# Third batch's attention weights and x turned by 32x32 blocks on VectorE instead of by TensorE, strided x copied in token order, and two weight pieces moved behind the sixth pair's copies

## The chip, the cores and the metric

One core of one Trainium2 chip. The metric is the device time of one execution in microseconds (us). Each time named as a result is a median of several executions; the rows of a profile come from one execution recorded by the hardware profiler.

## The reference

```python
def reference(q, k, v, g_ln, w_ch1, w_ch2):        # q, k, v: (B=8, H=8, S=576, D=64)
    stride = 32
    scores = (1.0 / np.sqrt(D)) * np.matmul(q, k.transpose(0, 1, 3, 2))
    rel = pos[:, None] - pos[None, :]
    mask_local = (rel >= 0) & (rel < stride)                       # heads 0 to 3
    mask_strided = (rel >= 0) & (pos[None, :] % stride == pos[:, None] % stride)   # heads 4 to 7
    scores = np.where(masks, scores, -1e9)
    attn = exp(scores - max); attn = attn / (sum(attn) + 1e-09)
    x = (attn @ v).transpose(0, 2, 1, 3).reshape(B, S, 512)
    mu, var = mean and variance of x over the last axis
    xn = (x - mu) / np.sqrt(var + 1e-06) * g_ln
    return x + np.maximum(xn @ w_ch1, 0.0) @ w_ch2                 # w_ch1: 512x2048, w_ch2: 2048x512
```

All arrays are fp32.

## The kernel before

**Split numbers.** Every operand of the feed-forward part is held as a high and a low part (`xh`/`xl`, `hh`/`hl`, two parts of each weight) in the fp32r format, and a product is three matmuls: high by high, high by low, low by high. The subtraction of the mean is folded into the first weights, and g_ln too.

**The attention** works on pairs of heads. A batch has four pairs, taken in the order local, strided, local, strided; pairs 8 to 11 are the third batch. Because of the masks only small blocks of scores exist: for a local pair 64 keys for each 32 queries, for a strided pair the tokens of one residue class, 18 by 18, in three classes at a time (54). `sm` holds the scores of a pair and later its softmax weights, with the query on the partition. To multiply by `v` the weights are needed with the key on the partition (`pt`), and the result `xo` (query on the partition) is needed with the channel on the partition (`xh`, `xl`) for the feed-forward part.

**Two ways of turning exist already.** Pairs 8 to 11 (`weights_and_x`, L678) are turned by TensorE: transposes of 128x128 tiles into a PSUM bank `px`, from which ScalarE copies `pt` and `xh`, and VectorE makes `xl`. From the fourth batch on the turn goes through DRAM: `spread` (L700) writes `sm` to a buffer `wd`, and `to_blocks` reads it back so that each 32x32 block stands in its final place but not turned; the same for x, which has gone to DRAM in any case (`xdl`, `xds`) and comes back as `sx`. One step of the loop later `turn_blocks` (L724) lets VectorE turn all blocks of a tile by one STREAM_TRANSPOSE; ScalarE makes `xh` from `sx`, VectorE `xl`, and the row sums follow.

**The order of the work.** TensorE runs its instructions in the order in which they are written. The start, about the first 100 us, follows a table, `ORDER`, for the first two batches: a letter and a pair (a, b, c, d of batch one, a1, b1, c1, d1 of batch two; b1 is the sixth pair), or a weight chunk such as `w3.lo0`, with an engine behind a slash where it matters. Here `C` is the copy of turned q or k from PSUM, `S` the scores, `E` the exponential, `P` the transposes of the weights, `F1` a feed-forward product; `w3.lo0` and `w3.sc0` are an ACT, a DVE and again an ACT instruction on half a chunk of w_ch1 (L229, L235).

After the table comes a loop of steps (run, f). A run is a batch with some of the 16 chunks f of the hidden layer: the second batch (`runs[1]`) with all 16, then the first batch with f = 8 to 15 (`runs[2]`), then the batches three to seven. Each step is: the first product of chunk f (L813, 12 matmuls), a slot, and the second product of the chunk before it (L838, 12 matmuls). In a slot the generator `visits` (L1067) may do one piece of attention work. `slots` says which steps have one: for the third batch before, f = 11 and 13 of the second batch's run and all eight steps of the first batch's rest.

A visit belongs to two pairs: the scores and softmax of pair i+1 and the values (product with `v`) of pair i, in one PSUM bank `sv` (`scores_and_values`, L614). For the third batch a visit had two pieces, `scores_and_values` and `weights_and_x`; from pair 12 on it has three: `scores_and_values` with `spread`, a piece with only loads, and `turn_blocks`.

`turn` (behind the second product of a step) turns q and k of the next pair and starts loads of the pair after: `load_half(0)` q, `load_half(1)` k, both on SyncE's queue. From pair 15 on k is loaded by ScalarE's queue behind `turn_blocks` instead.

`x_views` gives the pieces in which `x_high` (ACT, L599) and `x_low` (DVE, L604) copy a turned x. For a strided pair the PSUM bank holds the tokens by residue class, and they must come out in token order.

`x_t` gives two x buffers in turn; the third batch's is the one that the second batch used.

## Time and profile before

| | us |
|---|---|
| median of 3 executions (896.02 to 897.35) | 897.05 |
| the profiled execution | 897.86 |
| span of its records | 896.0 |
| TensorE matmul busy (PE) | 879.9 (98%) |
| VectorE busy (DVE) | 454.9 (51%) |
| ScalarE busy (ACT) | 241.6 (27%) |
| GpSimd busy (POOL) | 239.1 (27%) |

The profiled execution lies 0.81 us above the median; 1.86 us of it lie outside the span. PE is the matmul part of TensorE and PEld its weight load, which overlaps it. SP is SyncE, which mostly issues DMAs; ACTq and SPq are the queues' own records. All times below are microseconds from the start of the span.

### The profile page before, as it was taken

Reading aid. Unit: us, or ns where it says so; the run is one execution under the profiler, and the core shown is the slowest. Engines: PE = TensorE matmul, PEld = TensorE weight load, DVE = VectorE, ACT = ScalarE, POOL = GpSimd, SP = SyncE. Lnnn points to the kernel's source line nnn. Section 1 sums busy time; section 2 is a strip of 40 time slices with the busy share of each in tenths; the row PEclk is TensorE's granted clock in tenths of the full one; section 3 lists DMA queues with packets and bytes.
Section 4 is the critical chain, followed back from the end, with each engine's and each line's share of the span. In section 5 each row is a group of like instructions: output and inputs, shape, how many; then the busy total and the mean of one; then the engine's idle time right before and its main releaser. Section 6 shows DMA issues by size and latency. Waiting matters only on the chain.

```text
span 896.0 us, 18471 instructions
## 1 busy us (share of the span) xinstructions
PE 879.9 (98%) x7467; PEld 723.4 (81%) x7467; DVE 454.9 (51%) x855; ACT 241.6 (27%) x433; POOL 239.1 (27%) x293
## 2 busy tenths in 40 slices
PE   7889999999999999999999999999999999999998
PEld 5778888888888888888888888888888788888886
DVE  5887475346755455544645455546643754232400
ACT  4666465112211111111111111111122443333200
POOL 6768287110100010000100010001000468676000
PEclk9999999999999999999999999999999999999999
DMA  9989891117877565756485758575952001001210
GB/s 210 214 187 254 175 299 37 17 43 181 150 159 118 108 120 108 142 111 121 93 152 102 136 96 170 108 128 108 185 117 81 13 12 48 1 1 43 92 31 24
DMA packets 330973, 100.66 MB, mean 112 GB/s; under 512 B 269712, under 2 KB 321800, under 8 KB 330888
## 3 DMA queue, kind: packets, MB, share of 16 engines
q1 hardware_dynamic: 289704, 93.93, 47.2%
q10 hardware_dynamic: 41184, 5.54, 4.4%
q8 instruction: 59, 0.97, 0.5%
q14 instruction: 26, 0.21, 0.1%
HBM read 72.37 MB, written 27.06 MB: 111 GB/s over the span
## 4 chain that ended last, share of the span: by engine, by line
PE 93%; DMA 4%; SPq 1%; DVE 1%; ACT 1%; issue 0%; ACTq 0%
PE po L838 44%; PE ph L813 33%; PE u L1253 5%; PE sv L659 5%; PE v L1253 2%; DMA s<-in_moe_w_ch_dram 1%; PE c L1253 1%; DMA v_l<-in_v_dram 1%; DMA rows<-in_k_dram 1%; PE px L690 1%; DMA rows<-in_q_dram 1%; PE cm L270 0%; SPq L359 0%; PE pp L498 0%; SPq L412 0%; PE ph L968 0%
## 5 line engine op out<-in xcount | busy, mean ns | idle before, releaser
L838 PE MATMUL po<-w,hh 128*128 128x512 f32 x1024 | 320.3, 394 | 0.0
L813 PE MATMUL ph<-xh,w 128*128 128x512 f32 x880 | 290.5, 391 | 0.0
L838 PEld LDWEIGHTS po<-w,hh 128*128 128x128 f32 x1024 | 188.9, 188 | 39.3
L824 DVE SCALAR_TENSOR_TENSOR hl<-ph,hh 128x512 fp32r<-128x512 f32 x112 | 77.4, 692 | 263.5 <-ACT hh L819 263.5
L838 PE MATMUL po<-w,hl 128*128 128x512 f32 x512 | 199.4, 390 | 0.0
L813 PEld LDWEIGHTS ph<-xh,w 128*128 128x128 f32 x880 | 165.2, 188 | 34.5 <-DVE hl L824 0.2
L813 PE MATMUL ph<-xl,w 128*128 128x512 f32 x440 | 171.2, 389 | 0.0
L819 ACT ACTIVATE hh<-ph 128x512 fp32r<-128x512 f32 x112 | 66.8, 597 | 339.5 <-PE ph L813 298.9
L488 POOL TENSOR_TENSOR sm<-sm,mx 128x640 f32<-128x640 f32 (+1 forms) x32 | 40.6, 1270 | 343.7 <-issue 201.9
L838 PEld LDWEIGHTS po<-w,hl 128*128 128x128 f32 x512 | 96.1, 188 | 20.4
L813 PEld LDWEIGHTS ph<-xl,w 128*128 128x128 f32 x440 | 82.6, 188 | 16.8
L493 ACT ACTIVATE sm<-sm 128x640 f32<-128x640 f32 (+1 forms) x32 | 23.8, 743 | 104.7 <-POOL sm L488 104.7
L780 POOL TENSOR_TENSOR rs<-rs,mhalf 128x1 f32<-128x1 f32 x28 | 15.4, 552 | 121.6 <-DVE rs L779 95.5
L838 PE MATMUL po<-w,h 128*128 128x512 f32 x186 | 42.3, 389 | 0.0
L1120 POOL TENSOR_TENSOR sr<-sr,w 128x256 f32<-128x256 f32 x48 | 40.1, 836 | 3.8
L838 PEld LDWEIGHTS po<-w,h 128*128 128x128 f32 x186 | 34.9, 188 | 7.2
L1120 POOL TENSOR_TENSOR s<-sr,s 128x256 fp32r<-128x256 f32 x32 | 24.8, 803 | 25.3 <-ACT s L1239 25.3
L239 DVE SCALAR_TENSOR_TENSOR p<-s,p 128x512 uint32<-128x512 uint32 x32 | 22.0, 689 | 11.7 <-ACT p L235 11.2
L484 DVE TENSOR_REDUCE mx<-sm 128x10 f32<-128x640 f32 (+1 forms) x32 | 26.3, 823 | 1.9
L1120 DVE TENSOR_TENSOR x<-po,x 128x512 f32<-128x512 f32 x8 | 5.3, 689 | 39.6 <-PE po L838 29.9
L671 DVE TENSOR_TENSOR xo<-sv,den 128x256 f32<-128x256 f32 (+1 forms) x72 | 24.0, 390 | 0.0
L245 DVE SCALAR_TENSOR_TENSOR r<-s,p 128x512 uint32<-128x512 uint32 x32 | 21.9, 686 | 1.6
(195 smaller groups left out, 984.1 us busy)
## 6 DMA issues: line engine op xcount, KB each, us to landing
s<-in_moe_w_ch_dram SPq DMA_DIRECT2D x32, 512.0 KB
out_dram<-x SPq DMA_DIRECT2D x32, 256.0 KB
raw<-in_q_dram SPq DMA_DIRECT2D x104, 72.0 KB
raw<-in_k_dram ACTq DMA_DIRECT2D x68, 72.0 KB
v_l<-in_v_dram SPq DMA_DIRECT2D x32, 144.0 KB
x<-xdl SPq DMA_DIRECT2D x34, 128.0 KB
x<-xds SPq DMA_DIRECT2D x34, 128.0 KB
xdl<-xo SPq DMA_DIRECT2D x16, 256.0 KB
```

Source lines behind the costliest of these rows:

```text
L239: nc.vector.scalar_tensor_tensor(out=self.p[i], in0=self.bits(i), scalar=3, in1=self.p[i], op0=ALU.logical_shift_left, op1=ALU.bitwise_or)
L484: engine(self.mx[:, :, 0:nt], self.smv, axis=AX.X)
L488: nc.gpsimd.tensor_tensor(out=sm, in0=sm, in1=mx[:, :, 0:nt].unsqueeze(3).broadcast_to([P, 2, nt, w]), op=ALU.subtract)
L493: nc.scalar.activation(out=self.smv, in_=self.smv, func=AF.Exp, scale=SCALE)
L659: nc.tensor.matmul(dst, at, by, start=True, stop=True, tile_position=pos)
L671: nc.vector.tensor_tensor(out=xot[0:n, :, t0:t1], in0=src, in1=pv.den[0:n, :, t0:t1].unsqueeze(3).broadcast_to([n, 2, t1 - t0, D]), op=ALU ...
L813: nc.tensor.matmul(ph, w[:, cc], x[:, cc, :], start=(n + k == 0), stop=(n == NCC - 1 and k == 2))
L819: nc.scalar.activation(out=hh, in_=ph, func=AF.Relu)
L824: nc.vector.scalar_tensor_tensor(out=hl, in0=ph, scalar=0.0, in1=hh.bitcast(F32), op0=ALU.max, op1=ALU.subtract)
L838: nc.tensor.matmul(po, hx[:, cs], w, start=(start and n == 0), stop=(stop and n == 2))
L1120: engine.tensor_tensor(out=out, in0=a, in1=b, op=op)
L1253: nc.tensor.matmul(po, a[:, c], b[:, c, :], start=(start and c + k == 0), stop=(stop and c == 1 and k == 2), skip_group_check=True)
```

## The change

Four edits:

1. Pairs 8 to 11 (visits 7 to 11) now go the way of the later pairs: `spread`, and `turn_blocks` in a third piece. `weights_and_x` is gone. The slots become f = 9 to 15 of the second batch's run and the same eight steps behind it: 15 pieces, three a visit, where there were 10.
2. k of pairs 10 to 14 is loaded on ScalarE's queue behind `turn_blocks`, not on SyncE's.
3. `x_views` reads the strided pair's bank with a stride and writes `xh` and `xl` in token order; before it read nearly in order and wrote with a stride. Only the four strided pairs of the first two batches still use it.
4. In `ORDER`, `w3.lo0` and `w3.sc0` stand behind `C.qb1/ACT C.kb1/DVE` and `E.a1`. The rest of the table is the same, with other line ends.

```diff
 ORDER = """
...
-L.c1 w1.lw0 H.d Z.a1/DVE T.b1 w3.lo0 U.a1 Y.d F1.1.b w3.sc0 F1.1.a C.qb1/ACT C.kb1/DVE D.a1/POOL
-F1.0.d E.a1 w3.mg0 S.b1 w1.hi1 w3.sg0 w2.cm L.X4 P.a1 M.b1 w3.lo1 w3.bg F1.1.d L.vb1 G.a1 w2.ce
...
+C.qa1/ACT O.d w2.hi1 S.a1 L.Y3 w1.hi0 R.b1/POOL X.d M.a1 L.c1 w1.lw0 H.d Z.a1/DVE T.b1 U.a1 Y.d F1.1.b
+F1.1.a C.qb1/ACT C.kb1/DVE E.a1 w3.lo0 w3.sc0 D.a1/POOL F1.0.d w3.mg0 S.b1 w1.hi1 w3.sg0 w2.cm L.X4 P.a1
...
                 g = px[:, 0:P * NS].rearrange("p (g x) -> p g x", x=64)[:, :, 0:GS].rearrange(
-                    "p g (s t) -> p g s t", t=NB)[:, :, :, 0:n]
+                    "p g (s t) -> p t g s", t=NB)[:, 0:n]
...
-                    return x[:, cc, :].rearrange("p (t r) -> p r t", r=STR)
+                    return x[:, cc, :].rearrange("p (t r) -> p t r", r=STR)
...
-                if i < 3 * NHP + 2:
+                if i < 2 * NHP + 1:
                     pairs[i + 1].load_half(1)
...
             scores_and_values(pv, p)
-            by_blocks = i >= 3 * NHP
             px = pv if pv and pv.b + 1 < B else None
-            if by_blocks:
-                spread(px, p)
+            spread(px, p)
             turned(i + 2)
-            if by_blocks:
-                yield
+            yield
             if pv and i + 2 < NP:
                 pairs[i + 2].load_v()
             yield
-            (turn_blocks if by_blocks else weights_and_x)(px, p)
-            if by_blocks and i + 3 < NP:
+            turn_blocks(px, p)
+            if i + 3 < NP:
                 pairs[i + 3].load_half(1, nc.scalar)
             yield
...
-    LAST = 7
+    FIRST, LAST = 9, 7
...
-        slots[n] = (r is runs[1] and f in (11, 13) or r is runs[2]
+        slots[n] = (r is runs[1] and f >= FIRST or r is runs[2]
```

**The sixth pair.** On ACT, around the copies of b1's q (`qt_s`), before:

```order
L599 ACTIVATE xh_622<-px_3_867 128x30x16
L599 ACTIVATE xh_622<-px_3_867 128x2x16
L235 ACTIVATE p_3_902<-s_3_776 128x512
L229 ACTIVATE s_3_776<-s_3_776 128x512
L394 COPY qt_s<-t_2_891 128x32x16
L396 COPY qt_s<-tr_2_892 128x2x32
L493 ACTIVATE sm_200<-sm_200 128x2x5x64
L288 ACTIVATE w_1_949<-r_1_668 128x512
```

and now:

```order
L598 ACTIVATE xh_622<-px_3_867 128x16x30
L598 ACTIVATE xh_622<-px_3_867 128x16x2
L393 COPY qt_s<-t_2_891 128x32x16
L395 COPY qt_s<-tr_2_892 128x2x32
L492 ACTIVATE sm_200<-sm_200 128x2x5x64
L234 ACTIVATE p_3_917<-s_3_776 128x512
L228 ACTIVATE s_3_776<-s_3_776 128x512
L287 ACTIVATE w_1_949<-r_1_668 128x512
```

The two instructions on the weight chunk (`p_3`, `s_3`) moved behind three: the two copies of b1's q and the exponential of a1.

**The end of the second batch's run.** On ACT (with the numbers: `hh1_14` is chunk 14 of the second batch, `xh2` the third batch's x, `sm1`/`sm0` the weights of a local or strided pair), before:

```order
L819 ACTIVATE hh1_14_2458<-ph1_14_2445 128x512
L819 ACTIVATE hh1_15_2494<-ph1_15_2481 128x512
L819 ACTIVATE hh0_8_2525<-ph0_8_2512 128x512
L493 ACTIVATE sm0_199<-sm0_199 128x2x6x54
L819 ACTIVATE hh0_9_2637<-ph0_9_2624 128x512
L599 ACTIVATE xh2_2663<-px2_2_2652 128x512
L695 COPY pt2_2_2667<-px2_2_2652 128x768
```

and now:

```order
L796 ACTIVATE hh1_14_2550<-ph1_14_2537 128x512
L706 ACTIVATE xh2_2555<-sx2_0_2458 128x512
L347 DMA raw2_3_2509<-in_k_dram 32x18x32 x4
L796 ACTIVATE hh1_15_2600<-ph1_15_2587 128x512
L492 ACTIVATE sm1_200<-sm1_200 128x2x5x64
L796 ACTIVATE hh0_8_2714<-ph0_8_2701 128x512
```

The first write of `xh2`, with four loads of k behind it, now stands ahead of `hh1_15`; before it stood behind the run's last chunk. Its buffer was the second batch's x, which TensorE reads up to the product `ph1_15`.

What SP issues for the visit after it, now (`xds2` is x on its way to DRAM, `sx2` and `pt2` what comes back):

```order
L553 DMA xds2_213<-xo2_2_2670 54x6x128
L553 DMA xds2_213<-xo2_2_2670 54x5x128
L681 DMA wd1_220<-sm1_200 128x5x128
L699 DMA sx2_2_2677<-xds2_213 32x16x32 x4
L699 DMA pt2_1_2682<-wd1_220 32x20x32 x4
L347 DMA raw3_0_2720<-in_q_dram 32x18x32 x4
```

Of these the rows of `wd1`, `sx2` and `pt2` are new for the third batch, nine DMAs in such a visit.

**A piece of the third batch's weights.** On PE, at f = 9 of the first batch's rest, before:

```order
L813 MATMUL ph_9_2624<-xl_623,w_9_1863 128x512
L813 MATMUL ph_9_2624<-xh_622,w_9_1863 128x512
L690 MATMUL px_2_2652<-ident,xo_0_2594 128x128 x4
L690 MATMUL px_2_2652<-ident,sm_199 128x128 x6
L838 MATMUL po_8_0_2510<-w_8_1813,hh_8_2525 128x512 x2
```

and now at the place of such a piece (f = 14 of the second batch's run), and at the next slot:

```order
L790 MATMUL ph_14_2537<-xl_1066,w_14_2145 128x512
L790 MATMUL ph_14_2537<-xh_1065,w_14_2145 128x512
L815 MATMUL po_0_0_1685<-w_13_2099,hh_13_2503 128x512 x2
...
L790 MATMUL ph_15_2587<-xh_1065,w_15_2188 128x512
L658 MATMUL sv_1_2604<-v_s,pt_2_2463 64x64 x22
L658 MATMUL sv_1_2604<-kt_l,qt_l 32x64 x36
```

The transposes (`px`) are gone from PE, 47 in the five pieces together; the `sv` pieces stand at f = 9, 12 and 15 of the second batch's run and f = 10 and 13 of the first batch's rest. Else PE's order is the same.

## Rows read from the trace of the kernel before

**Rows 1.** The page's first part: busy time, share of the span and instructions of each engine.

```profile
PE 879.9 (98%) x7467; PEld 723.4 (81%) x7467; DVE 454.9 (51%) x855; ACT 241.6 (27%) x433; POOL 239.1 (27%) x293
```

**Rows 2.** The page's chain of work that ended last, shares by engine.

```profile
PE 93%; DMA 4%; SPq 1%; DVE 1%; ACT 1%; issue 0%; ACTq 0%
```

**Rows 3.** The chain, third batch's pieces: start, us, what.

```profile
177.36 0.55 PE px L690 x5
...
201.67 1.09 PE px L690 x10
...
215.65 1.20 PE px L690 x11
```

**Rows 4.** The chain again, around the sixth pair.

```profile
37.90 7.08 DMA s<-in_moe_w_ch_dram
...
45.00 0.62 ACT p L235
...
47.64 0.91 PE sp L457 x44
...
54.90 0.66 PE pp L498 x6
```

**Rows 5.** PE's and ACT's waits from 40 to 48: total, times, longest.

```profile
PE sp L457 <- DVE kt_s L396: 2.3, 1, 2.3
...
ACT p L235 <- DMA s<-in_moe_w_ch_dram: 2.0, 1, 2.0
```

**Rows 6.** Busy time in stretches.

```profile
core 0: us, PE busy (x) PEld busy (x) DVE busy (x) ACT busy (x) POOL busy (x), PEclk, DMA share, GB/s
47.60:52.40 4.80, 4.76 (x131) 3.95 (x134) 4.10 (x7) 2.76 (x5) 3.80 (x5) 0.64 0.79 135
194.10:250.00 55.90, 55.90 (x698) 46.49 (x698) 39.96 (x80) 14.28 (x22) 7.29 (x8) 1.00 0.69 146
602.20:620.50 18.30, 18.30 (x216) 15.01 (x202) 10.51 (x19) 3.06 (x5) 1.26 (x1) 1.00 0.68 133
```

**Rows 7.** Timeline of POOL and ACT around 50: start, us, engine, operation, idle before.

```profile
46.04 2.23 POOL L401 COPY v_l<-v_l 32x1088 f32<-32x1088 f32 x2 [1.75 <-DMA v_l<-in_v_dram]
49.12 1.04 POOL L253 TENSOR_TENSOR wg<-r,gcol 128x512 f32<-128x512 f32 x1 [0.84 <-DVE r L245]
...
51.47 1.27 POOL L488 TENSOR_TENSOR sm<-sm,mx 128x648 f32<-128x648 f32 x1
...
52.78 0.75 ACT L493 ACTIVATE sm<-sm 128x648 f32<-128x648 f32 x1 [0.81 <-POOL sm L488]
```

**Rows 8.** Groups by form, first 105 us: count, busy us, mean ns, idle before.

```profile
L599 ACT ACTIVATE xh<-px 128x480 fp32r<-128x480 f32 x4 | 4.3, 1066 | 1.8 <-PE px L559 1.6
...
L599 ACT ACTIVATE xh<-px 128x512 fp32r<-128x512 f32 x4 | 2.4, 597 | 2.3 <-PE px L559 2.3
L388 ACT COPY kt_l<-t 128x512 f32<-128x512 f32 x3 | 1.8, 594 | 6.7 <-PE t L377 6.7
```

**Rows 9.** Timeline, two visits of a later batch with block turns.

```profile
597.32 0.97 DVE L731 STREAM_TRANSPOSE pt<-pt 128x768 f32<-128x768 f32 x1
...
598.63 4.64 ACTq L348 DMA_DIRECT2D raw<-in_k_dram  x4
...
600.73 0.91 PE L659 MATMUL sv<-v_s,pt 54*64 54x64 f32 x44
...
603.38 0.60 ACT L819 ACTIVATE hh<-ph 128x512 fp32r<-128x512 f32 x1 [5.32 <-DMA v_l<-in_v_dram]
...
617.62 0.84 DVE L731 STREAM_TRANSPOSE pt<-pt 128x640 f32<-128x640 f32 x1 [1.42 <-DMA pt<-wd]
...
619.01 0.97 PE L659 MATMUL sv<-v_l,pt 64*32 64x64 f32 x72
```

**Rows 10.** DVE's waits from 590 to 670.

```profile
DVE pt L731 <- DMA pt<-wd: 5.2, 3, 2.3
```

**Rows 11.** Timeline, loads of k at an earlier visit.

```profile
270.82 2.00 ACTq L348 DMA_DIRECT2D raw<-in_k_dram  x4
```

More of the change, by code (lines that the diff above doesn't have):

```diff
@@ L676, in scores_and_values @@
             pv.x_store(whole=False)
-    def weights_and_x(px, p):
-        ps = bank(f"px{p.id if p else px.id}")
-        n_x = 0
-        turns_x, turns_p = [], []
-        if px:
-            n_x = NT if px.local else NS
-            turns_x = [(t, px.xov[:, t]) for t in range(n_x)]
-        if p:
-            turns_p = [(n_x + t, p.sm[:, t].rearrange("p h x -> p (h x)")) for t in range(p.nt)]
-        k = -n_x % NT
-        for t, src in turns_p[:k] + turns_x + turns_p[k:]:
-            nc.tensor.transpose(ps[:, P * t:P * (t + 1)], src, ident)
-        if px:
-            px.x_parts(ps)
-        if p:
-            p.pt = smp.tile([P, NS, P], F32, tag="pt", name=f"pt{p.id}")
-            nc.scalar.copy(out=p.pt[:, 0:p.nt].rearrange("p t x -> p (t x)"),
-                           in_=ps[:, P * n_x:P * (n_x + p.nt)])
-            p.row_sums()
-            p.inverse()
     def spread(px, p):
```

45 lines of the change are left out of this document (22 added, 23 removed).

## The prediction

> **What bounds the kernel now.** First the page's busy times [rows 1]: TensorE's matmuls fill 98% of the span, no other engine much over half. The chain of work that ended last says the same of its length: 93% PE, the rest almost all in the first hundred microseconds, where the loads set the pace [rows 2]. Next, the place of the change. In the stretch from 194.1 to 250.0, which holds most of the third batch's pieces, PE is busy 55.90 of 55.90 us at a granted clock of 1.00 (of 2.4 GHz), with the DMA engines busy 0.69 [rows 6]. So there a matmul taken off PE's list shortens the run by its own time, and VectorE, busy 39.96 us, and the DMAs cost something only where PE comes to wait for them. Around the sixth pair it is otherwise: PE stands idle for 2.3 us until the copy of `kt_s` is there, and just before, ACT has stood idle for 2.0 us until a weight chunk lands [rows 5]. These are the two places to price. The sum is made for the profiled execution (897.86, span 896.0) and its difference carried to the median, 897.05, 0.81 lower; a difference under 0.2% (1.8 us) I call none, as that is about what a measurement of this kernel can tell.
>
> **Term 1: the transposes.** The 47 px transposes of five pieces stand on the chain as five pieces of it: 0.55 us for five of them, 1.09 for ten, 1.20 for eleven [rows 3]; the last two sizes come twice (two more pieces, like these two). 0.55 + 2 x 1.09 + 2 x 1.20 = 5.13 us. Nothing is put on PE in their place. The `sv` pieces move, but are as many and as long. PE's saving here is **5.1 us**; it could be less only by waits, which are term 4.
>
> **Term 2: the sixth pair.** Before, ACT waits 2.0 us for the weight chunk, whose landing ends 7.08 us of DMA that began at 37.90, does its two instructions (0.62 and about as much), and only then copies b1's q; VectorE copies b1's k after that, and PE's scores of b1 start at 47.64 [rows 4, 5]. With the chunk's two instructions behind, the copies of q and k can go while the chunk is still on its way, and the scores start up to 2.3 us earlier. Behind the idle time the granted clock is 0.64 from 47.6 to 52.4 [rows 6]; at full clock that stretch of 4.8 us would be 4.8 x 0.64 = 3.1, another 1.7 us. So the gain lies between 0 (something else ends last) and 2.3 + 1.7 = 4.0. What is late next is GpSimd: two copies of `v_l`, which wait for a DMA and end at 46.04 + 2.23 = 48.27, three weight instructions that take 51.47 - 49.12 = 2.35 us, b1's subtraction, 1.27 us, and then ACT's exponential, 0.75 us [rows 7]. Packed without a gap they end at 48.27 + 2.35 + 1.27 + 0.75 = 52.64, and b1's weights can be transposed then, at 52.7 in place of 54.90 [rows 4]. I take 54.9 - 52.7 = **2.2 us**. The 2.3 and the 1.7 don't add past this point, because GpSimd's start hangs on a DMA that the change doesn't touch. The moved weight instructions are hardly late: the three that pass them run mostly in the 2.0 us in which ACT waited for the chunk.
>
> **Term 3: x in token order.** Before, a copy of 480 elements a partition takes ACT 1066 ns, one of 512 without a stride on either side 597 [rows 8]; VectorE's copies differ alike. If the stride of the write is what costs, each of the four large copies on each engine gets about 0.47 us shorter. If the strided read costs the same again, nothing is gained; a strided read may also cost more. The nearest row is a copy that reads PSUM with a stride and writes without one (`kt_l`, L388): 594 ns [rows 8]. I go by it. But none of the eight lies on the path: at the only one near it, b1's (d before it), PE's later work waits for loads, and the copies of the other pairs end long before their use. The term is **0**, and up to 1 us either way if the price of a read with a stride is far from that row.
>
> The Trainium skill, "SBUF — State Buffer", section "Door 1: The DMA port swizzle (why `[64,N]` ≈ `[32,N]`)", says the opposite of the row: PSUM is read in lines of 8 bytes, so that an access to it that isn't contiguous slows matmuls down, where SBUF forgives a stride of up to 4 fp32 values. If the rule holds for copies too, edit 3 would move the stride to the dearer side and save nothing; by the row it saves 0.47 us a copy. The sum is the same by either, and L388's 594 ns disagrees with the rule.
>
> **Term 4: the trip through DRAM.** The five visits now take three steps each, and each has a round trip: exponential, write of `sm`, read in blocks, VectorE's turn, which must be done before the next `sv` piece. No visit of the third batch shows it in the trace, but the last batches do it at the same distance of 18.3 us with the DMA engines busy 0.68, nearly the 0.69 here [rows 6]. There the local pair's turn ends at 617.62 + 0.84 = 618.46 and the `sv` piece starts at 619.01: 0.55 us to spare. The strided pair's ends at 597.32 + 0.97 = 598.29, `sv` at 600.73: 2.4 to spare [rows 9]. VectorE does wait for `pt`, three times, 2.3 us at most [rows 10], PE not. So at the later batches' pace the trip costs nothing. VectorE's added turns, 0.84 to 0.97 us each for the weights and no longer for x, which is smaller, have cover: it is busy 40 of 55.9 us in the third batch's stretch [rows 6, 9].
>
> One wait is new. `xh2`'s buffer is read by PE up to `ph1_15`, so at visit 8 ACT stands until that product is done, and behind it stand four loads of k and `hh1_15`; VectorE waits for `xh2`, and the next visit's masking stands behind that. The loads of k take ACT's queue from 2.00 us [rows 11] to 4.64 [rows 9]. ACT's `hh` then starts 0.6 + 2.0 = 2.6 to 0.6 + 4.64 = 5.2 us after `ph1_15`'s end, which is where `sv` starts; at the visit of before it came 603.38 - 600.73 = 2.65 after [rows 9]. The softmax of that visit is so 0 to 2.6 us later than at that visit, and with 0.55 to spare the next `sv` waits 0 to 2.0 us. `hl` is made at the latest 5.2 + 0.6 + 0.7 = 6.5 us after, and PE needs it only behind an `sv` piece of 1.7 and two products of 2.7, 7.1. I take **0.5**, near the lower end, because the loads of k two steps ahead of a busy weight stream look like the short ones.
>
> **Sum.** -5.1 - 2.2 + 0 + 0.5 = -6.8 us. 897.86 - 6.8 = 891.1 for an execution like the profiled one, 897.05 - 6.8 = **890.3** as the median.
>
> **The rivals.**
>
> *The head's gain is given back.* The chain up to there is made of loads of weights, and the share of the DMA engines is 0.79 from 47.6 to 52.4 [rows 6]. If the next chunk sets the time at which PE can go on, the 2.2 us become a wait some microseconds later. Against it: behind 54.90 the chain goes on through PE's own work, not through a load. The time would be 892.5. Chance 0.18.
>
> *A PSUM read with a stride is dear.* Then ACT and VectorE take as long as before or longer in the four pairs; if each of the two pairs whose copies come in this stretch then holds the path up by 0.5 us, the time is 891.3. Chance 0.10.
>
> *The trip is too long (the other side).* The block writes and reads move in pieces of 128 bytes, and with the third batch they come at a time when x of the second batch is fetched and its output is stored. If the trip takes longer than at the later visits by d us, the two local visits cost d - 0.55 each and the two strided d - 2.4 each, 4d - 5.9 in all, and the gain of 7.3 is used up at d = 3.3. At d = 4 it is 10 us, and the time 897.05 - 7.3 + 10.1 = 900. For it: of the three visits of rows 10 one has VectorE wait 2.3 us for `pt`, so the trip has no slack, and SP takes its DMAs in order, `pt` behind the loads of `sx`, which wait for x's own store. Against it: the share of the DMA engines is the same, and the k loads leave SP. Chance 0.22, of which half ends above 898.85.
>
> The Trainium skill, "DMA: Bandwidth & Descriptors", section "Specifications", gives 512 bytes as the least transfer for full rate; the pieces here have 128, which makes this rival a little more likely. The visits of rows 9 make the trip in time with such pieces.
>
> *That the change doesn't do what it says* is excluded for term 1: PE's new order has none of the transposes.
>
> **How the numbers follow.** My own case has 0.50, with a range of its own of 888.0 (head 4.0 in place of 2.2, no wait) to 892.2 (a wait of 2.0, head 1.8). The given-back head 0.18, dear reads 0.10, the long trip 0.22. What leaves out about two in ten is 887.0 to 896.0: below, a head that gains the whole 4.0, no wait and 1 us from the copies; above, the long trip up to d near 3. Faster by over 0.2% (below 895.25): the first three cases, 0.78, and the mild end of the trip, 0.03: 0.81. No difference (895.25 to 898.85): 0.08. Slower: 0.11.
>
> **What would show it.** The rows of px at L690 are gone, and PE is still without a gap from 160 to 250: term 1. PE's wait for `kt_s` at the sixth pair is gone or below 0.5 us, the clock there is nearer 1, and b1's transposes start near 52.7, with no new wait up to 70: term 2; if they come early and a wait for a weight chunk follows, the first rival. Copies `xh` of 480 near 600 ns: term 3; near 1000 or more, the second. PE waits for `pt` at `sv` in the third batch by 0.5 us, in the visit behind `ph1_15` and there alone: term 4; waits at all four, the third rival. The prediction is wrong if the trip is longer than at the later visits, or if what PE gains in the head is not the whole head's gain.

## The result, and the profile after

The changed kernel is slower: 901.39 us against 896.9 in the same runs, a ratio of 1.0058 [1.0038, 1.0078]. The forecast was 890.3. The profiled execution of it took 908.72, 7.3 above its median; 4.3 us of its distance to the profiled execution of before lie in the start, ahead of 97 us, and are not part of what follows.

The page's busy times and the chain by engine, after:

```profile
PE 883.2 (97%) x7420; PEld 724.3 (80%) x7420; DVE 459.4 (51%) x862; ACT 235.0 (26%) x426; POOL 238.7 (26%) x293
...
PE 70%; DMA 2%; DVE 2%; SPq 2%; issue 1%; ACT 1%; POOL 0%; ACTq 0%; DVEq 0%
```

PE has 47 instructions fewer than in [rows 1], as the change says, but it is busy longer, and the chain, 93% PE in [rows 2], is 70%. Busy time by stretches shows where (the columns are those of [rows 6]); first after:

```profile
core 0: us, PE busy (x) PEld busy (x) DVE busy (x) ACT busy (x) POOL busy (x), PEclk, DMA share, GB/s
180.00:250.00 70.00, 64.96 (x599) 52.30 (x598) 42.55 (x85) 10.61 (x17) 8.38 (x10) 0.98 0.82 162
250.00:300.00 50.00, 48.01 (x420) 39.16 (x419) 26.68 (x49) 7.53 (x12) 3.63 (x4) 0.97 0.71 134
...
235.00:245.00 10.00, 6.84 (x62) 5.26 (x50) 5.24 (x13) 0.97 (x2) 1.81 (x2) 0.90 1.05 173
...
243.00:247.00 4.00, 4.00 (x12) 3.10 (x11) 2.21 (x7) 1.33 (x2) 1.51 (x2) 0.57 0.69 215
...
260.00:264.00 4.00, 4.00 (x84) 3.36 (x67) 1.25 (x3) 0.60 (x1) 0.00 (x0) 0.57 0.67 91
```

and before, the same stretch:

```profile
180.00:250.00 70.00, 70.00 (x760) 57.94 (x760) 43.12 (x88) 15.47 (x24) 8.39 (x10) 1.00 0.57 123
```

PE was never idle there and now is for 5.0 + 2.0 = 7.0 us, and behind two of the idle times the granted clock is 0.57 in a stretch of 4 us (243 to 247, 260 to 264), at the lower of its two levels (1.2 of 2.4 GHz) for most of it: 2 x 4 x 0.43 = 3.4 us more. The share of the DMA engines has gone from 0.57 to 0.82; from 194.1 to 250, the stretch of [rows 6], it has gone from 0.69 to 0.84. Between two marks that both kernels have, the last pair of transposes of strided x in the table (93.00, now 97.32) and one in the tail (717.26, now 728.16), it is 630.84 in place of 624.26: 6.6 us longer, though 5.1 us of transposes are gone. So some 11.7 us are lost in that execution, of which idle time and clock explain 10.4; the rest stays unassigned. In the median it is 4.5 + 5.1 = 9.6.

A visit of the third batch in the timeline (start, us, engine, operation, and in brackets the idle time before it and what ended it). It is the visit of pair 11's values and pair 12's scores, the slowest. Pair 12 is the first of the fourth batch, but its weights too were turned by TensorE before:

```profile
233.42 1.11 PE L658 MATMUL sv<-v_s,pt 54*64 54x64 f32 x44 [1.64 <-issue]
...
235.43 4.63 ACTq L347 DMA_DIRECT2D raw<-in_k_dram  x4
...
240.16 0.60 ACT L796 ACTIVATE hh<-ph 128x512 fp32r<-128x512 f32 x1 [9.46 <-DMA raw<-in_k_dram]
...
241.54 0.50 PE L790 MATMUL ph<-xh,w 128*128 128x512 f32 x1 [3.16 <-DVE hl L801]
...
244.21 0.73 SPq L553 DMA_DIRECT2D xds<-xo  x2
...
245.38 0.39 SPq L681 DMA_DIRECT2D wd<-sm  x1
...
250.84 1.90 SPq L699 DMA_DIRECT2D sx<-xds  x4
...
252.84 2.08 SPq L699 DMA_DIRECT2D pt<-wd  x4
...
257.24 0.84 DVE L708 STREAM_TRANSPOSE pt<-pt 128x640 f32<-128x640 f32 x1 [1.74 <-DMA pt<-wd]
...
258.71 0.50 PE L790 MATMUL ph<-xl,w 128*128 128x512 f32 x1 [1.99 <-DVE xl L710]
...
259.38 1.05 PE L658 MATMUL sv<-v_l,pt 64*32 64x64 f32 x72
```

The trip from the `sv` piece to the turned `pt` takes 257.24 + 0.84 - 233.42 = 24.7 us; for the local pair's weights of [rows 9] it was 618.46 - 600.73 = 17.7. Two things are longer. ACT can't make `hh`, which stands behind the loads of k, until 6.7 us after `sv` (2.65 in [rows 9]), so the masking and all behind it are 4.1 us late. And SyncE reads back later. It asks for `pt` 252.84 - 245.38 = 7.5 us behind the store of the weights (`wd`), against 613.55 - 608.68 = 4.9 at the visit of before, and for x 250.84 - 244.21 = 6.6 us behind x's own store, against 611.54 - 607.49 = 4.05 (these rows are of the kernel before):

```profile
582.45 0.97 PE L659 MATMUL sv<-v_l,pt 64*32 64x64 f32 x72
...
607.49 0.73 SPq L554 DMA_DIRECT2D xds<-xo  x2
...
608.68 0.39 SPq L704 DMA_DIRECT2D wd<-sm  x1
...
611.54 1.90 SPq L722 DMA_DIRECT2D sx<-xds  x4
...
613.55 2.07 SPq L722 DMA_DIRECT2D pt<-wd  x4
```

4.1 + 2.6 are 6.7 of the 7.0. The second part is mostly the landing: in the trace the store of the weights has landed 6.4 us after its issue, where it took 3.7 at the visit of before, and `pt` is asked for 1.1 us after that.

The first part comes from how the two queues are tied together. The DMAs of SyncE and ScalarE signal their landing on eight semaphores, handed out in turn, and in the trace none of them starts before the one ahead of it on the same semaphore has landed (823 of 823 cases). So the four loads of k here start at 235.43, 236.53, 237.48 and 239.75, each within 0.1 us of the landing of one of SyncE's loads (of x, q, q and v), though they read nothing of it. On SyncE's queue a load of x waits in the same way, for one of v (SyncE's waits from 180 to 300):

```profile
SPq L747 <- DMA v_l<-in_v_dram: 2.2, 1, 2.2
```

The three visits ahead of the slowest took 15.8 (a strided pair's weights), 18.8 (local) and 20.0 (strided; from 176.15, 194.45 and 213.33); a strided pair's took 598.29 - 582.45 = 15.8 in the kernel before. PE is held at three places: at an `sv` piece (1.64), at a first product whose PSUM is not yet freed by `hl` (3.16), and at the first product of the third batch itself, which needs the `xl` of the last pair (1.99). That `xl` stands on VectorE behind the turn of `pt`, which waits 1.74 us for its load.

ACT's waits from 180 to 300 (total, times, longest):

```profile
ACT hh L796 <- PE ph L790: 37.9, 11, 5.4
...
ACT hh L796 <- DMA raw<-in_k_dram: 24.1, 4, 9.5
```

The token-order copies, by form, in the first 105 us (count, busy us, mean ns, idle before):

```profile
L603 DVE TENSOR_TENSOR xl<-px,xh 128x480 fp32r<-128x480 f32 x4 | 2.6, 654 | 0.5 <-ACT xh L598 0.5
...
L598 ACT ACTIVATE xh<-px 128x480 fp32r<-128x480 f32 x4 | 2.3, 576 | 2.6 <-PE px L558 2.4
```

576 ns in place of the 1066 of [rows 8].

### The profile page after: what moved, and what is told of

Read it like the earlier page. It is cut to its first block, busy times and chain, and to the rows that moved or that the text cites. A ratio compares the mean times of both kernels' runs of the same rounds, so it can differ in the third digit from the quotient of the medians.

```text
span 906.8 us, 18455 instructions
## 1 busy us (share of the span) xinstructions
PE 883.2 (97%) x7420; PEld 724.3 (80%) x7420; DVE 459.4 (51%) x862; ACT 235.0 (26%) x426; POOL 238.7 (26%) x293
## 4 chain that ended last, share of the span: by engine, by line
PE 70%; DMA 2%; DVE 2%; SPq 2%; issue 1%; ACT 1%; POOL 0%; ACTq 0%; DVEq 0%
PE po L815 34%; PE ph L790 23%; PE u L1227 5%; PE sv L658 4%; PE v L1227 2%; PE c L1227 1%; SPq L699 1%; DMA xds<-xo 1%; SPq L347 1%; DMA v_l<-in_v_dram 1%; DMA xdl<-xo 0%; DMA v_s<-in_v_dram 0%; DMA pt<-wd 0%; DVE xr L1094 0%; DVE x L877 0%
## 5 line engine op out<-in xcount | busy, mean ns | idle before, releaser
L1094 POOL TENSOR_TENSOR s<-sr,s 128x256 fp32r<-128x256 f32 x32 | 24.7, 799 | 25.5 <-ACT s L1213 25.5
L708 DVE STREAM_TRANSPOSE pt<-pt 128x640 f32<-128x640 f32 (+1 forms) x24 | 21.2, 882 | 8.9 <-DMA pt<-wd 8.9
```

The source lines that it names most:

```text
L1094: engine.tensor_tensor(out=out, in0=a, in1=b, op=op)
```

## The experiments

**Theories.** A: ScalarE, held by the loads of k, is the cause. E: SyncE, held at x's reading back by x's own store, with pt, q and v behind it. F: everything lands late because the DMA engines are at 0.8 there. G: VectorE waits for rows of the residual that land late. I: A, E and G hand the delay on to each other. B is the other one of e2, C and D are the two of e5 and e6, H is the other one of e13. The median of before is that measured beside the run. PE's idle time and granted clock are read from the stretch 180 to 300 of each run's one profile; the last column is the time between the two marks in that profile, less the 624.26 of before.

| run | third batch | median (before) | ratio [95%] | PE idle, us | clock | marks, us |
|---|---|---|---|---|---|---|
| e1 | as changed | 901.05 (897.14) | 1.0044 [1.0031, 1.0057] | 7.6 | 0.99 | +8.0 |
| e2 | k on SyncE | 904.03 (897.14) | 1.0085 [1.0065, 1.0106] | 6.7 | 0.96 | +6.3 |
| e3 | before, with the table | 897.38 (897.14) | 1.0015 [1.0000, 1.0030] | 0 | 1.00 | -0.1 |
| e4 | before, with token order | 896.46 (897.14) | 0.9997 [0.9986, 1.0009] | 0 | 1.00 | -0.1 |
| e5 | x alone by blocks | 897.63 (896.64) | 1.0010 [0.9998, 1.0022] | 2.4 | 1.00 | +2.05 |
| e6 | weights alone by blocks | 900.79 (896.64) | 1.0032 [1.0016, 1.0048] | 3.3 | 1.00 | +1.0 |
| e7 | q, k in large pieces | 899.72 (896.64) | 1.0036 [1.0024, 1.0049] | 5.2 | 0.99 | +3.6 |
| e8 | pt before x on SyncE | 909.56 (896.64) | 1.0136 [1.0120, 1.0152] | 12.3 | 0.97 | +15.7 |
| e9 | e5, k on SyncE, pt's copy first | 899.77 (897.02) | 1.0030 [1.0013, 1.0046] | 1.2 | 1.00 | +0.9 |
| e10 | e8, and on VectorE | 909.17 (897.02) | 1.0141 [1.0118, 1.0164] | 8.0 | 0.96 | +12.55 |
| e11 | no wait for x's store | 898.62 (897.02) | 1.0025 [1.0010, 1.0039] | 4.7 | 0.99 | +2.1 |
| e12 | x a step later | 904.02 (897.02) | 1.0079 [1.0057, 1.0101] | 9.1 | 0.97 | +7.2 |
| e13 | rows later | 904.76 (897.55) | 1.0087 [1.0057, 1.0117] | 7.4 | 0.97 | +7.5 |
| e14 | e9, rows later | 900.11 (897.55) | 1.0023 [1.0005, 1.0042] | 1.9 | 0.99 | +3.3 |
| e15 | e2, rows later | 904.30 (897.55) | 1.0076 [1.0053, 1.0099] | 8.4 | 0.94 | +8.9 |
| e16 | e14, old table | 900.62 (897.55) | 1.0021 [1.0001, 1.0041] | 1.1 | 1.00 | +1.8 |
| e17 | e11, k on SyncE, rows later | 902.40 (896.81) | 1.0055 [1.0035, 1.0075] | 5.4 | 0.96 | +4.1 |
| e18 | blocks in two visits of five | 896.61 (896.81) | 0.9996 [0.9982, 1.0010] | 0 | 1.00 | -1.5 |

A profile is of one execution: that of e1 is 7.8 us slower than its median, that of e11 4.4 slower, that of e6 4.3 faster. The idle time alone doesn't give the time: e2 and e17 stand less than e1 and take longer, at a lower clock.

**e1, the changed kernel again.** No edit.

> The changed kernel a second time, for a profile whose first 40 us are like those of before (in the first one PE had done 1.6 us less by 40 us, at a clock of 0.83 in place of 0.96). All theories: a median near 901.4; between 180 and 300 PE stands still for 6 to 7 us that it did not before, at the sv pieces of the third batch and what follows them. On the sixth pair: if the head's gain was kept, PE's scores of b1 start by 45.5 us and the third batch's first sv piece comes some 2 us earlier than before; if it was given back, that piece comes at the same time as before or later.

901.05: the result stands, and the waits are at the same places (7.6 us). The profiled execution had the late start once more (the mark of 93.00 at 96.10), so on the sixth pair it says nothing.

**e2, k on SyncE.**

```diff
-                if i < 2 * NHP + 1:
+                if i < 3 * NHP + 2:
                     pairs[i + 1].load_half(1)
...
-            if i + 3 < NP:
+            if i >= 3 * NHP and i + 3 < NP:
                 pairs[i + 3].load_half(1, nc.scalar)
```

> The changed kernel with one part undone: k of pairs 10 to 14 is loaded on SyncE's queue again, as in the kernel before, instead of ScalarE's. Theory A (ScalarE is held by the four loads of k, whose issue has to wait for earlier loads, and with it hh, the masking, the exponential and so the weights' trip): ScalarE's idle time that ends with a load of k, 24 us in 180 to 300, is gone, PE's waits there fall from 7 us to under 1.5, and the time is 890 to 894. Theory B (SyncE's queue takes too long for the visit's loads, x's own store and the weights among them, wherever k is): four more DMAs of about 0.5 us each stand on SyncE's queue, pt lands as late or later, PE waits 6 to 10 us, and the time is 900 to 904.

904.03. ACT's waits for k go from 24 us to 2.9, as theory A wants, and PE waits as long as before (6.7 us). What takes their place, in VectorE's and PE's timeline:

```profile
242.38 0.69 DVE L752 BATCH_NORM_STATS2 st<-x 128x6 f32<-128x512 f32 x1 [4.29 <-DMA x<-xds]
...
244.81 0.68 DVE L801 SCALAR_TENSOR_TENSOR hl<-ph,hh 128x512 fp32r<-128x512 f32 x1
...
245.55 0.80 PE L790 MATMUL ph<-xh,w 128*128 128x512 f32 x1 [3.64 <-DVE hl L801]
```

Rows of the residual land late, VectorE waits for them 4.3 us, and `hl` stands behind. Theory A alone is out.

**e3, the table alone, on the kernel before.**

```diff
-Z.a1/DVE T.b1 w3.lo0 U.a1 Y.d F1.1.b w3.sc0 F1.1.a C.qb1/ACT C.kb1/DVE D.a1/POOL
-F1.0.d E.a1 w3.mg0
+Z.a1/DVE T.b1 U.a1 Y.d F1.1.b F1.1.a C.qb1/ACT C.kb1/DVE E.a1 w3.lo0 w3.sc0 D.a1/POOL
+F1.0.d w3.mg0
```

> The kernel before with the change of the order table alone (w3.lo0 and w3.sc0 behind the sixth pair's copies). If the head's gain is kept, as the prediction had it: 2.2 us less, 894.7, with b1's scores some 2 us earlier and no new wait. If it is given back or is no gain: 896.0 to 898.0, with PE's wait moved to some other place before 70 us.

897.38 against 897.14: no gain. PE's waits from 40 to 62 in e3 (total, times, longest):

```profile
PE av L513 <- ACT pt L502: 1.4, 1, 1.4
PE po L837 <- DVE hl L823: 1.0, 1, 1.0
```

The wait of 2.3 us for `kt_s` [rows 5] is gone, and 1.4 + 1.0 = 2.4 have come. The timeline of ACT, VectorE and GpSimd says why:

```profile
45.76 0.63 ACT L234 ACTIVATE p<-s 128x512 uint32<-128x512 uint8 x1
46.33 0.65 ACT L228 ACTIVATE s<-s 128x512 f32<-128x512 f32 x1
46.89 0.62 ACT L287 ACTIVATE w<-r 128x512 fp32r<-128x512 f32 x1
...
47.83 0.69 DVE L244 SCALAR_TENSOR_TENSOR r<-s,p 128x512 uint32<-128x512 uint32 x1
...
48.55 0.64 ACT L234 ACTIVATE p<-s 128x512 uint32<-128x512 uint8 x1 [1.05 <-DVE r L244]
48.67 1.04 POOL L252 TENSOR_TENSOR wg<-r,gcol 128x512 f32<-128x512 f32 x1 [1.08 <-DVE r L244]
49.12 0.69 ACT L502 COPY pt<-pp 128x640 f32<-128x640 f32 x1
...
55.61 0.67 ACT L228 ACTIVATE s<-s 128x512 f32<-128x512 f32 x1 [1.76 <-DMA s<-in_moe_w_ch_dram]
```

The first two rows are the moved instructions, both ACT's; VectorE makes `r` from what they write (in the pieces `w3.mg0` and `w3.sg0`, which have not moved). Two things wait for `r`: ACT's next weight instruction, with a1's copy of `pt` behind it, and GpSimd's first weight instruction, with b1's softmax behind it. GpSimd's starts at 48.67 and had started at 49.12 [rows 7]: 0.45 us are won there, not 2.2. PE comes to a1's values earlier and waits for `pt`; later ACT waits 1.76 us for the next weight chunk, and `hh` and `hl` stand behind that.

The profiles of the other runs say the same. The mark of 93.00 lies at 92.7 in the mean of the sixteen with the new table (90.0 to 97.3) and at 92.8 in that of the four with the old one.

**e4, token order alone, on the kernel before.**

```diff
-                    "p g (s t) -> p g s t", t=NB)[:, :, :, 0:n]
+                    "p g (s t) -> p t g s", t=NB)[:, 0:n]
```

(and the two views of `tok` and `parts` as in the change.)

> The kernel before with the token-order copies alone (strided read of PSUM, writes without a stride). By the row of L388: the four ACT copies of 480 elements take about 0.6 us in place of 1.07, and the time is the same, 896 to 898. If a strided read of PSUM is as dear as a strided write: 1.07 us or more, and the time the same or up to 1 us longer.

896.46 against 897.14, 0.9997: the copies of 480 elements take 571 ns on ACT, and the time is the same. In this run's profile, PE's wait for `kt_s` is 1.3 us with the old table, where [rows 5] have 2.3: the start varies from one execution to the next by more than the swap was to gain.

**e5 and e6, one half each.** `weights_and_x` is back; in the third batch it gets the weights alone (e5) or x alone (e6), behind `turn_blocks` for the other.

```diff
+            third = i < 3 * NHP
-            spread(px, p)
+            spread(px, None if third else p)
...
-            turn_blocks(px, p)
+            turn_blocks(px, None if third else p)
+            if third:
+                weights_and_x(None, p)
```

> The changed kernel, but in the third batch only x goes by blocks through DRAM; the weights are turned by TensorE again (27 of the 47 transposes back, in the third piece of a visit). Theory C (the cost is the weights' trip: PE needs pt one step after it is asked for, and the DMA engines, 0.8 busy there, and SyncE's queue, where pt stands behind x's own store and its reading back, bring it too late; x itself has until the next run): no PE wait over 0.5 us from 170 to 310, 20 transposes saved, 20 x 0.11 = 2.2 us, and a time of 894 to 896. Theory D (ScalarE held by loads of k, whatever is turned how, delays hh and hl): the waits behind hl stay, 3 us or more, and the time is 897 to 900.

897.63 against 896.64. PE waits 1.41 us for ACT's copy of `pt` (which stands behind `xh2`, and that for `ph1_15`) and 0.98 for `hl`: the 2.2 us of the transposes are spent. Theory C has no wait over 0.5 us here, and theory D 3 us or more behind `hl`; neither is met.

> The other half: in the third batch only the weights go by blocks, x is turned by TensorE again (20 of the 47 transposes back). Theory C: the trip stays on the path, but without x's reading back ahead of it on SyncE's queue and with less traffic; PE waits 2 to 5 us from 170 to 310, 27 x 0.11 = 2.9 us are saved, and the time is 896 to 900. If it was the reading back of x alone that made pt late, the waits are gone and the time is 894.

900.79. The waits seen are 1.8 and 1.4 us:

```profile
PE ph L812 <- DVE hl L823: 1.8, 1, 1.8
PE sv L658 <- DVE xl L603: 1.4, 1, 1.4
```

The first comes behind 4.2 us in which VectorE waits for rows; the second is this run's own (`sv` and `px` share one PSUM buffer). With no x ahead of `pt`, SyncE still waits up to 5.7 us for the weights' own store. Set against what each saves, the medians say: x by blocks costs 1.0 + 2.2 = 3.2, the weights 4.15 + 2.9 = 7.0, both together 9.0 (e1, 3.9 + 5.1). But e6's executions lie between 896.49 and 903.53, and the profiled one is the fastest of them; from mark to mark it is 2.05 + 2.2 = 4.25 and 1.04 + 2.9 = 3.9. So each half costs what it saves or more; which costs more, and whether the two add up, isn't shown.

**e7, q and k in large pieces.** In the third and fourth batch, q and k are loaded by as many DMAs of as many bytes, in pieces of 2304 bytes; the elements of q and k are then in another order.

```diff
+                    if self.b in (2, 3):
+                        queue.dma_start(
+                            self.raw[p0:p0 + 32, i],
+                            src[self.b, self.h0 + h].rearrange("(t g) d -> t (g d)", t=32)[
+                                :, S * d:S * d + S])
+                        continue
```

> The changed kernel with q and k of the third and fourth batch loaded in pieces of 2304 bytes, not 128, as many bytes by as many DMAs; their layout is then another, so those two batches compute with q and k in a wrong order. If the load on the DMA engines by small pieces is what makes the trip late (theory C, first half): the DMA share from 180 to 250 falls from 0.80 to under 0.7, k's loads no longer hold ScalarE for 4 us, PE's waits fall from 7 us to under 2, time 892 to 895. If it is the order and the chain of DMAs on SyncE's queue (second half): waits of 5 us or more stay, 898 to 901.

899.72. The stretch in question:

```profile
180.00:250.00 70.00, 66.08 (x601) 52.63 (x600) 43.67 (x84) 9.92 (x17) 7.09 (x9) 0.98 0.72 159
```

The DMA share is 0.72 in place of 0.80 (e1), PE idles 5.2 in place of 7.6 us, and the distance to before is 3.1 us in place of 3.9, a difference within the two intervals. ACT still waits 22.9 us for loads of k. A part of the loss may go with the load of small pieces; most does not.

**e8 and e10, pt ahead of x.** In e8 on SyncE's queue in `spread`, in e10 also on VectorE:

```diff
+        if p:
+            p.pt = smp.tile([P, NS, P], F32, tag="pt", name=f"pt{p.id}")
+            p.sp = p.pt[:, 0:p.nt].rearrange("p t x -> p (t x)")
+            to_blocks(p.sp, d[0:p.nt * P].rearrange("(j c) x -> c j x", c=32))
         if px:
             cs = P * px.n0
...
         if px:
-            nc.vector.transpose(px.sx, px.sx)
...
+        if p:
+            nc.vector.transpose(p.sp, p.sp)
+        if px:
+            nc.vector.transpose(px.sx, px.sx)
```

> The changed kernel with the four loads of pt put ahead of the four of sx on SyncE's queue, in all visits. If pt is late because it stands behind the reading back of x, which waits for x's own store (3.6 to 6.3 us to land): pt is asked for 2 us earlier or more, PE's waits fall from 7 us to 2 to 4, and the time is 895 to 898. If the landing of the weights' own store is as late, or the loads of k hold ScalarE: 900 to 902.

> As e8 (pt's loads ahead of x's reading back on SyncE), and VectorE turns pt ahead of x too, in all visits. In e8 VectorE stood 12.6 us for sx with pt landed behind it. If that order on VectorE was what made e8 8 us slower than the changed kernel: PE no longer waits at an sv piece, and the time falls below 901; if x's late landing holds VectorE in the same way, only behind pt, and with it hl: PE's waits stay at the first products, 5 us or more, and the time is 901 to 908.

909.56 and 909.17, the worst of all. VectorE's waits from 180 to 300 in e8:

```profile
DVE sx L704 <- DMA sx<-xds: 6.7, 2, 4.5
DVE sx L704 <- DMA sx<-xdl: 5.9, 2, 4.2
```

and SyncE's:

```profile
SPq L699 <- DMA wd<-sm: 23.0, 6, 5.2
```

`pt` now stands first on the queue, and SyncE waits for the weights' own store, up to 5.2 us, as the second theory of e8 had it. x lands late, VectorE stands for it, and behind it `hl`. With pt first on VectorE too (e10) it stands for the rows (6.6 us) and for `xh` to make `xl` (6.0), and PE still waits 2.0 us at an `sv` piece and 5.3 for `hl`. One queue's gain is the next one's loss. Both edits are in all visits, and some 3 us of PE's idle time in e8 and 2.5 in e10 come between 600 and 700.

**e9, x by blocks with its two waits removed.** e5 with pt's copy ahead of `xh`, and k as in e2.

```diff
+            if third:
+                weights_and_x(None, p)
-            turn_blocks(px, p)
+            turn_blocks(px, None if third else p)
```

> As e5 (in the third batch only x goes by blocks, the weights are turned by TensorE), with two waits taken out: ACT's copy of pt stands ahead of xh, which waits for the last product that reads its buffer (1.41 us of PE in e5), and k of pairs 10 to 14 is loaded on SyncE's queue as in the kernel before (ACT stood 7 us behind loads in e5, and PE 0.98 behind hl). If these are the waits of e5: none is left in the third batch, 2.2 us are saved, 894.4 to 895.4. If x's traffic alone makes hl late by another way (the residual's rows land later and VectorE waits for them): a wait of 1 us or more stays, and the time is 896 to 898.

899.77. Both waits are gone, one of 1.24 us for `hl`, behind rows, has come, and one of 1.1 between 600 and 700: no gain again.

**e11, no wait for x's store.** The third batch's x is read from the second's, into a buffer of its own, so it is another x.

```diff
-            t = smp.tile([P, NS, 2, D], F32, tag="xo", name=f"sx{px.id}")
+            b_x = px.b - (px.b == 2)
+            px.sx = tkp.tile([P, DM], F32, tag="tk", name=f"sx{px.id}")
...
-                xd_l[px.b][0:CH, cs:cs + P].rearrange("(j c) d -> c j d", c=STR) if px.local else
+                xd_l[b_x][0:CH, cs:cs + P].rearrange("(j c) d -> c j d", c=STR) if px.local else
```

> The changed kernel, but in the third batch sx is read from the batch before's x, which has long been stored, into a buffer of its own, so that it doesn't wait for x's own store (and the third batch's x is another one). The number of DMAs and bytes is the same. Theory E (SyncE's queue is held at sx by x's store, 1.3 to 5.5 us a visit, and pt, q and v stand behind it, and k on ACT behind these): pt lands 2 us or more earlier, ACT's waits for k fall below half of 24 us, PE's waits from 7.7 to under 3, time 893 to 896. Theory F (the landing of everything is slow under a DMA share of 0.8, with eight DMAs in flight at most): less than 2 us of it goes, 899 to 901.

898.62, 1.6 us over before where the changed kernel is 3.9 over (e1). In its profile no `sv` piece waits for pt any more; the waits left, 3.20 and 1.23 us, are for `hl`, behind ACT's loads of k:

```profile
ACT hh L800 <- DMA raw<-in_k_dram: 22.6, 4, 9.2
```

So theory E holds for some 2.3 us of 9 by the medians, and falls as the whole. At the slowest visit `pt` is still asked for 6.7 us behind the store of the weights.

**e12, x a step later.** `sx` is read in the second piece, when its store has landed, and turned at the head of the next visit.

```diff
+            if held:
+                turn_blocks(held.pop(), None)
             scores_and_values(pv, p)
...
+            if third:
+                x_blocks(px)
```

> The changed kernel with x's reading back of pairs 8 to 10 moved a step later (into the second piece, when its store has landed) and its turn, xh and xl into the next visit's first piece; pt stays where it was. The output is the reference's. Theory E: SyncE is held by nothing but the weights' own store, pt comes in time, PE's waits fall to under 2.5, time 892.5 to 895.5. Theory F: the waits stay at 5 us or more, 899 to 902.

904.02. Its longest wait, 6.22 us for `hl` at 246.4, comes behind VectorE's turn of `sx`, which waits 2.67 us for its load, and the softmax behind that, for which ACT stands ahead of `hh`. At the step before, ACT stands up to 10.1 us for loads of q, which x has joined on the queue.

**e13 to e16, rows later.** The use of the residual's rows two steps later, in the changed kernel (e13), e9 (e14), e2 (e15), and e9 with the table of before (e16).

```diff
-                loads, scales = [i] * (0 <= i < NT), [i - 2] * (1 < i <= NT + 1)
+                loads, scales = [i] * (0 <= i < NT), {13: [0], 14: [1], 15: [2, 3]}.get(f, [])
```

> The changed kernel with one thing moved: the statistics of the first two batches' residual rows (VectorE's L752 and what follows) stand at steps f = 13, 14 and 15 instead of 11 to 14, their loads where they were. Theory G (VectorE stands for rows that land late, and hl behind them holds PE): PE's waits from 170 to 310 fall from 7.7 us to 4 or less, 896 to 898.5. Theory H (the loads of k on ACT are what makes hl late in this kernel, the rows only where k is on SyncE): the waits stay at 6 us or more, 900 to 902.

> As e9 (x alone by blocks, k of pairs 10 to 14 on SyncE, pt's copy ahead of xh) with the statistics of the residual's rows at steps 13 to 15. Its one wait in e9, 1.24 us of PE for hl at 239.6, came behind 3.6 us of VectorE for such rows. Theory G: no wait is left in the third batch, and 20 transposes, 2.2 us, are gained: 894 to 896 beside 896.9 of before. If x's traffic costs by another way: 897 to 900 as in e9.

> As e2 (the changed kernel with k of pairs 10 to 14 on SyncE) with the statistics of the residual's rows at steps 13 to 15. Theory G: the wait of 3.64 us for hl at 245.5 is gone, the two for pt, 0.86 and 2.21, stay: 897 to 899 in place of 904. If hl is late by another thing: 902 to 904.

> As e14 with the order table of before (w3.lo0 and w3.sc0 ahead of the sixth pair's copies). By e3 the table is worth nothing: the same time as e14 within 1 us. If the swap costs on its own (e3's interval reaches 0.3%): 1 to 2 us less than e14, 893 to 894.5.

904.76, 900.11, 904.30, 900.62: nothing is won. VectorE no longer waits for rows in any of the four; in e15 the wait of 3.64 us is gone and 2.40 (`xh`) and 2.05 (`xl`) stand at the first product of the third batch. Theory G falls. e14 and e16 differ by 0.5 us, so the table is worth nothing here either.

**e17, three holds at once.** e11 with the edits of e2 and e13, and so with another x.

> The changed kernel with three holds taken away at once: sx is read from the batch before's x into a buffer of its own (so the third batch's x is another one), k of pairs 10 to 14 is loaded on SyncE, and the residual's statistics stand at steps 13 to 15. As many DMAs and bytes as the changed kernel. Theory I (three in-order queues each hand the delay on, so only all three together help): PE's waits from 170 to 310 fall under 1.5 us, 892 to 895. Theory F (the landing times under a DMA share of 0.8 are the cause): waits of 3 us or more stay, for pt, and the time is 897 to 900, near e11's 898.6.

902.40. No `sv` piece waits, no load of k holds ACT for more than 2.9 us, no rows hold VectorE; and at the first product of the third batch:

```profile
242.75 4.87 SPq L703 DMA_DIRECT2D sx<-xds  x4
...
249.50 0.71 DVE L708 STREAM_TRANSPOSE sx<-sx 128x512 f32<-128x512 f32 x1 [5.09 <-DMA sx<-xds]
250.25 0.63 ACT L710 ACTIVATE xh<-sx 128x512 fp32r<-128x512 f32 x1 [6.56 <-DVE sx L708]
...
250.93 0.79 PE L794 MATMUL ph<-xh,w 128*128 128x512 f32 x1 [3.18 <-ACT xh L710]
...
252.24 0.85 DVE L712 STREAM_TRANSPOSE pt<-pt 128x640 f32<-128x640 f32 x1 [2.02 <-DMA pt<-wd]
253.01 0.65 DVE L714 TENSOR_TENSOR xl<-sx,xh 128x512 fp32r<-128x512 f32 x1
```

The four DMAs of `sx` take SyncE 4.87 us (1.90 in the slowest visit above), and x of the last pair comes 3.2 us late. PE waits 2.0 us more for `xl`, which stands on VectorE behind the turn of `pt`: `pt` is late after all, though no `sv` piece waits for it. Theory I falls. Theory F's waits of 3 us or more are there, but the time is above its forecast too; the clock is 0.96.

**e18, blocks in the first two visits alone.**

```diff
+            by_blocks = i <= 2 * NHP or i >= 3 * NHP
+            if by_blocks:
+                spread(px, p)
...
-            turn_blocks(px, p)
+            (turn_blocks if by_blocks else weights_and_x)(px, p)
```

(with the table of before, the token order, and k as in e2.)

> The order table of before; blocks in the first two of the third batch's five visits alone (before 200 us, where the DMA engines were hardly busy before), TensorE's transposes in the other three, k on SyncE as before. 15 of the 47 transposes go: 0.55 + 1.09 = 1.6 us. If the load of the later visits is the cause: no PE wait in the third batch, 895.0 to 895.8 beside 896.9 of before. If every trip through DRAM in three steps costs here: 897 or more.

896.61 against 896.81, 0.9996 [0.9982, 1.0010]: in time no difference that can be told. In the profile:

```profile
180.00:250.00 70.00, 70.00 (x756) 57.86 (x755) 42.57 (x87) 13.34 (x23) 7.11 (x9) 1.00 0.62 129
```

PE has no gap and the clock is 1.00; the DMA share is 0.62. From mark to mark (91.83 to 714.63) it is 622.80 us against 624.26, 1.46 less, where 15 transposes are worth 1.64; e3 and e4, with the third batch of before, lie within 0.12 of the 624.26. So the trip by blocks can be hidden in three steps here, where the load is small: from 160 to 200 the DMA share is 0.13 before and 0.65 in e18.

## Why the prediction was wrong

**Term 1, the transposes, 5.1 us: right as a mechanism.** The rows of px at L690 are gone, and e18, the one run without waits, shows 15 of them come off PE's path at nearly their own time in its one profile. The whole 5.1 was never seen free of waits.

**Term 2, the sixth pair, 2.2 us: wrong; nothing is gained.** The scores started earlier and the wait for `kt_s` went, as said, but e3 shows 2.4 us of new waits. The step that failed is "what is late next". It packed GpSimd's weight instructions without a gap behind `v_l`, though their row shows a wait of 0.84 us for `r` [rows 7], and `r` is made from what the moved instructions write. And it did not ask what else waits for `r`: ACT's next weight instruction, and behind it a1's copy of `pt`. The first rival has the outcome right, but its reason, a late weight chunk, accounts for 1.0 of the 2.4 us. "The moved weight instructions are hardly late" was nearly true (0.76 us) and beside the point.

**Term 3, the copies: right.** The row of L388 decided, 576 ns and no change in time; the rule of the Trainium skill, "SBUF — State Buffer", section "Door 1: The DMA port swizzle (why `[64,N]` ≈ `[32,N]`)", which says that a PSUM access that isn't contiguous slows matmuls, does not carry over to these copies: 576 ns with a strided read, 1066 with a strided write.

**Term 4, the trip, 0.5 us: wrong by about 9, and it decides.** The trip is too long, as the third rival had it, but it costs in other places. The rival charged a local visit with d - 0.55 us and a strided one with d - 2.4, where d is by how much the trip is longer than at the later visits. Against later visits of the same kind (17.7 local, 15.8 strided) the four measured trips are longer by 0 (strided), 1.1 (local), 4.2 (strided) and 6.9 (local). For the first three the charges are 0, 0.55 and 1.8 us, and PE stands 0, 0.23 and 1.64 at these `sv` pieces. For the last the charge is 6.35, and PE doesn't stand at that `sv` piece at all, because it has already stood 3.16 us for `hl` and 1.99 for `xl` on the way. So the sum of the charges, 8.7, is near the loss of 9.0 to 9.6 partly by luck, and the rival's own sign, waits at all four, was not seen.

The step that failed is the one that took the later visits' pace for this one, by which the trip "costs nothing" and the rival was put at 0.22: "the share of the DMA engines is the same", 0.68 there and 0.69 here. The 0.69 is that of the kernel before, without the trips' own traffic; with it the share is 0.84 in the same stretch, and 1.05, as the profile counts it, in the worst ten microseconds. The visits of [rows 9] have their traffic already in their 0.68. Here it came on top of the second batch's output, the residual's rows of two batches, and q, k and v. The share was also the wrong measure: in e7 it is 0.72 and PE stands 5.2 us, in e5 0.64 and it stands 2.4. What sets this visit apart is the landing. From the store of pair 12's weights to their reading back it is 4.9 us at the visit of [rows 9], 7.5 in the changed kernel, and 6.0 to 8.8 in all eleven other runs that send these weights by blocks, whatever was taken away.

Smaller steps went wrong with it. The sum asked for pt at `sv` alone; `xl` of the last pair, which VectorE makes behind the turn of `pt`, is needed by the third batch's first product, and PE waits for it in the changed kernel (1.99 us), e13, e15 and e17. The loads of k took ACT's queue 4.63 us at the slowest visit, within the price of 2.00 to 4.64; but ACT had stood 4.7 us before the first of them could start, and `hh` came 6.7 us after `sv` in place of 2.6 to 5.2. And the wait for `ph1_15`, which was priced as the new one, is there (ACT stands 4.8 us for it) and cost PE next to nothing in the changed kernel.

**What is settled and what is open.** Shown: the loss is the third batch's trips, since the table and the copies alone cost at most 0.3% (e3, e4) and no wait is left where two of the five visits alone go by blocks (e18). Each half of the trip costs what it saves or more; x's store that holds SyncE is worth 2.3 us by the medians. Not the cause by itself: k on ACT, the order of pt and x, the residual's rows, and with x's store all three together (e17); each such edit moved the wait to the next engine that works in order. Open: why a store takes so long to land there. While that of pair 12's weights does (245 to 252), the DMA engines are busy 0.50 and no more; they are busy 1.05 in the ten microseconds ahead. That the DMA load is the reason was not shown by a run that takes the load away and leaves the order. No run gives the two queues semaphores of their own, either. No version tried beats the kernel before by more than can be measured; e18 comes out even.

## What to carry to other kernels

When work is moved from a full engine to DMAs, a DMA share read before the change is the wrong number: add the new traffic, and compare with a stretch that already carries it. Compare also how long a store takes to land, and what each DMA has to wait for before it may start; the share tells neither. A round trip through DRAM has as many places to be late as there are queues that work in order behind it, so ask for each engine what stands behind the waiting instruction, and who first needs every product of the trip, not only the one that is asked for soonest. When an instruction is moved out of the way of one, look what it is now in the way of.

## What the runs showed of the hardware

The granted clock fell behind idle times of 3.16 and 1.99 us in the middle of a busy stretch (0.57 from 243 to 247 and from 260 to 264), and not behind one of 1.64 us (1.00 from 233 to 238). So a wait of PE can cost more than its length: 7.0 us of idle time came with 3.4 us at the lower clock. The same store of a local pair's weights landed 3.7 us after its issue at a later visit and 6.4 us at the slowest visit of the third batch. And putting loads that are needed sooner ahead of others on one queue, in all visits, made the kernel 8 us slower (e8), not faster.
